# Top-k attention and a leaky-ReLU layer on one core: the sign bit of the weights' rounding on GpSimd, early units transposed on TensorE, and a chunk's first layer begun ahead

## The chip, the cores and the metric

The kernel runs on one core of a Trainium2 chip. The metric is the device time of one execution in microseconds, the median of three runs. The profile is of one further execution, recorded instruction by instruction; its span is the time from the first to the last instruction.

## The reference

Eight batches of eight heads, 576 queries and keys of width 64. Each query keeps its 32 largest scores, the rest are masked, and the softmax weighs the values. The heads are put side by side into 4608 tokens of width 512, which go through two layers with a leaky ReLU between them.

```python
scores = scale * np.matmul(q, k.transpose(0, 1, 3, 2))          # scale = 1/8
kth = np.partition(scores, -32, axis=-1)[..., -32:-31]
scores = np.where(scores >= kth, scores, -1e9)
attn = softmax(scores)                                          # + 1e-9 in the divisor
x = (attn @ v).transpose(0, 2, 1, 3).reshape(4608, 512)
h = x @ w_in                                                    # 512 -> 2048
out = np.maximum(0.01 * h, h) @ w_out                           # 2048 -> 512
```

The two weight matrices come as 64-bit floats; everything else is 32-bit.

## The kernel before

**Rounding the weights.** The weights are loaded as sixteen pieces of 128 x 1024 numbers of four 16-bit words each (tile `raw`, three buffers, issued on the SP queue, L102) and rounded to 32-bit floats on the chip. `round_weights` (L104) is a generator in three stages, and the driver (L484 on) runs stage one of piece n, stage two of piece n-1 and stage three of piece n-2 in turn. Stage one: GpSimd copies the top word out (`top`, L119, two buffers), ScalarE turns the middle and the low words into floats (L120, L122). Stage two: VectorE makes the exponent in `scale` (L124, L126), ScalarE shifts it into place (L128; for the last two pieces VectorE, L130), VectorE makes the top part of the mantissa (`m_top`, in a buffer of the tile `wT`, L131) and keeps the sign bit alone in `top` (L132); TensorE sums the three parts in PSUM (L142 to L144). Stage three: VectorE joins exponent and sign (L146) and multiplies (L149). The loads of the first queries and keys stand between those of the pieces in the SP queue. Top-k of the first unit follows the last piece on VectorE.

**Attention.** Two heads make a pair, four pairs a batch. A unit is 128 rows of queries of one pair (both heads), or, for the 64 rows left over, of two pairs; there are 144 units. A step s works on several units at once: top-k of unit s on VectorE (`top_k`: L244, then four rounds of MAX8 at L249 and of match and replace at L252), the mask of unit s-1 on GpSimd (`mask`: L260, L262, L263), its exponentials and row sums on ScalarE (L266, L271), the reciprocals of unit s-2 on VectorE (L275), its normalizing on ScalarE (L278) and its transposition, and every second step the scores of units s+2 and s+3 on TensorE (`scores`: L214, copied out by ScalarE at L221). Each engine works through its instructions in the order in which the program issues them.

A unit is transposed in one of two ways. `transpose` has ScalarE split the words into two tiles (`split`, L287, two buffers), which go out to DRAM (`apart`, L288) and come back by a transposing DMA (L290). `transpose_in_haste` does nine TensorE transposes into two buffers of the PSUM tile `wide` (L300), which ScalarE copies to `wT` (L306); this is for the units in HURRIED, 15, 23 and 31. The values of two units are weighed together on TensorE (L327), at the place that `values_at` names: step n+4, MIDDLE, for an odd unit n below 14 and its even neighbour, step n+3, END, for later ones, one step sooner for those in HURRIED. ScalarE copies the result into `x` (L341).

**The two layers.** Tokens go in chunks: two of 128, then seventeen of 256. A chunk becomes ready at the place where the values of its last unit are copied. `mlp` (L366) is a generator that yields a cost after every few products. For the 128-token chunks `hidden_of_few` (L345) computes the first layer with the tokens stationary, in four blocks of 512 (L352), and turns each block with four transposes after the next block (L362). For the others the first layer is eight times two tiles of 128 hidden units, each summed over the four pairs (L378), with the activation on ScalarE (L384). The second layer is L390. `mlp_steps` pulls products out of the generators up to a budget, in seven slots of each step (EARLY_SHARE = 500 a slot until the first 256-token chunk is ready, later the backlog spread over the steps until the next chunk is ready). So the feed-forward products are laid between the attention products in TensorE's order.

The units of batch 0 go by query tile first, then by pair. So units 0 to 3 complete the first chunk, 4 to 7 the second, 8 to 15 the third, which is the first of 256 tokens.

```python
            late = s < HURRY and not {s - 1, s - 2} & set(HURRIED)
            if older and not late:
                weights_of(older)
            mlp_steps(budget)
            weighed = values(s, MIDDLE)
```

`weights_of` is the reciprocals and the normalizing; with `late` they come one slot of top-k later.

Of the kernel before, what the change touches and what calls it, by code (L numbers as in the profile page):

```python
# [19 lines left out]
def kernel(  # L20
# [73 lines left out]

    def load_weights(n):
        if n >= NPIECE:
            return
        if not AS_WORDS:
            nc.sync.dma_start(piece(n), weights[n])
            return  # L100
        raw_of[n] = raws.tile([P, WCH, 4], U16, name="raw")
        nc.sync.dma_start(raw_of[n].rearrange("p n w -> p (n w)"), weights[n])  # L102

    def round_weights(n):  # L104
# [14 lines left out]
        nc.gpsimd.tensor_copy(top, raw[:, :, 3])  # L119
        nc.scalar.activation(dst, mid, AF.Copy, bias=-7.0 - 2.0 ** -16, scale=2.0 ** -20)  # L120

        nc.scalar.activation(m_low, low, AF.Copy, bias=128.0, scale=2.0 ** -29)  # L122
        yield
        nc.vector.tensor_scalar(scale, top, 4, 0x7FF, ALU.logical_shift_right, ALU.bitwise_and)  # L124

        nc.vector.tensor_scalar(scale, scale, 1151.0, 896.0, ALU.min, ALU.max)  # L126
# [5 lines left out]
        nc.vector.tensor_scalar(top, top, 0x8000, None, ALU.bitwise_and)  # L132
# [13 lines left out]
        nc.vector.tensor_tensor(scale, scale, top, ALU.bitwise_or)  # L146
# [42 lines left out]
    for b in range(B):  # L189
        first = b % 2 == 1  # L190
        whole = [Unit(b, [b * HP + hp], q0 + LEFT * first)
                 for q0 in range(0, S - LEFT, P) for hp in range(HP)]
# [30 lines left out]
    def first_scores(u):  # L223

        ps = [ps_sc.tile([P, 2, 512], F32, name="wide", bufs=2) for i in range(2)]
        for half in range(2):
            for i, pi, side, r0 in u.parts:
                qt, kt = qk_of[pi]
                d = slice(side * D, (side + 1) * D)
                nc.tensor.matmul(ps[i][:, half, 0:HS], qt[d, u.q0:u.q0 + P],  # L230
# [114 lines left out]
    def hidden_of_few(x):  # L345

        g_of = {}
        for j in range(NFC // 4 + 1):
            if j < NFC // 4:
                ph = ps_ml.tile([P, 512], F32, name="ph", tag="ml")  # L350
                for c in range(HP):
                    nc.tensor.matmul(ph, x[c][:, 0:P], w_in[c][:, j * 512:(j + 1) * 512],  # L352
                                     start=(c == 0), stop=(c == HP - 1))
                    if c == 1:
                        yield 2 * 512
                g_of[j] = raws.tile([P, 2 * DMODEL], U16, name="scale", bufs=2).bitcast(F32)
                nc.scalar.activation(g_of[j], ph, AF.Prelu, alpha=SLOPE)
                yield 2 * 512
            if j:
                pt = ps_ml.tile([P, 4, P], F32, name="pt", tag="ml")  # L360
                for i in range(4):
# [270 lines left out]
```

## Time and profile before

| | us |
|---|---|
| median of three runs | 1476.7 (1475.35 to 1476.87) |
| the profiled execution, its span | 1473.8 |
| TensorE busy with products | 1393.5 |
| VectorE busy | 1328.3 |
| ScalarE, GpSimd busy | 1096.2, 1097.7 |
| first top-k instruction (L244) | 68.7 |
| last VectorE instruction (L275) | 1395.4 |
| products after the last values (L378, L390) | 1414.9 to 1473.8 |

A product of 32-bit floats is two records in the trace. In a stretch without waits, records of L378 start 0.219 us apart, those of L390 and L352 0.429 us. The recorded end of a matmul is modelled, so busy time of TensorE includes some waiting.

In the lines of the profile, a group reads: source line, engine, operation, output <- inputs, shapes and count, then busy time and the mean of one in ns, then idle time of the engine just before these instructions with what ended it. A piece of the chain reads: start, duration, engine, output and line.

### The profile page before, as it was taken

To read this page: it belongs to the slowest core of one execution; us is meant where nothing else is said; L and a number is where in the kernel's file an instruction comes from. 1 tells how busy PE (TensorE), PEld (TensorE's weight loads), DVE (VectorE), ACT (ScalarE), POOL (GpSimd) and SP (SyncE) were. 2 spreads that over 40 slices of the span, in tenths; PEclk is the share of its full clock that TensorE was granted. 3 is DMA by queue.
4 is the path that set the end of the run, shared out by engine and by line. 5 is a ranking of instruction groups with operands and counts; after the bars stand their busy time and mean duration, and the time that the engine had idled before them with its cause. 6 is when DMAs were issued, how large, how long until landed. Compare 5 with 4: busy or idle time off the path is not lost.

```text
span 1473.8 us, 24093 instructions
## 1 busy us (share of the span) xinstructions
PE 1393.5 (95%) x8057; PEld 927.6 (63%) x8059; DVE 1328.3 (90%) x3414; ACT 1096.2 (74%) x1979; POOL 1097.7 (74%) x742
## 2 busy tenths in 40 slices
PE   6716989999999999999999999999999999999998
PEld 2304547676766666666666666767676767676674
DVE  7999999999999999999999999999999999999600
ACT  8647887777787777777777777787877787877710
POOL 2278887888788888788878887888788888787700
PEclk9957999999999999999999999999999999999999
DMA  9724453655367554666466545565557555554510
GB/s 331 298 64 127 131 153 102 175 157 148 105 166 206 142 146 129 180 181 150 135 167 189 155 125 147 165 196 142 130 165 207 138 141 132 165 135 135 144 47 14
DMA packets 391421, 223.48 MB, mean 152 GB/s; under 512 B 336256, under 2 KB 336257, under 8 KB 389249
## 3 DMA queue, kind: packets, MB, share of 16 engines
q1 hardware_dynamic: 391296, 221.95, 53.6%
q8 instruction: 63, 1.03, 0.3%
q14 instruction: 62, 0.50, 0.1%
HBM read 46.14 MB, written 92.60 MB: 94 GB/s over the span
## 4 chain that ended last, share of the span: by engine, by line
PE 81%; DVE 14%; DMA 2%; ACT 2%; issue 1%; SPq 0%; POOL 0%; DVEq 0%; ACTq 0%
PE pz L390 31%; PE ph L378 30%; PE wide L327 10%; PE wide L214 6%; DVE tops L249 5%; DVE pairs L252 4%; PE narrow L214 3%; DVE pairs L244 1%; DMA wT<-apart 1%; ACT split L287 1%; DVE w_out L149 1%; DVE w_in L149 1%; DVE scale L146 1%; DVE scale L124 0%; ACT s_sb L278 0%
## 5 line engine op out<-in xcount | busy, mean ns | idle before, releaser
L262 POOL TENSOR_SCALAR pen<-s_sb,tops 128x576 f32<-128x576 f32 x288 | 638.3, 2216 | 207.7 <-DVE tops L249 120.2
L249 DVE MAX8 tops<-pairs 128x8 f32<-128x288 f32 (+1 forms) x1152 | 635.9, 591 | 0.0
L390 PE MATMUL pz<-w_out,gT 128*128 128x512 f32 x1152 | 508.4, 596 | 0.0
L378 PE MATMUL ph<-x,w_in 128*128 128x256 f32 x2176 | 481.1, 381 | 0.0
L252 DVE MATCH_REPLACE8 pairs<-tops,pairs 128x288 f32<-128x288 f32 (+1 forms) x864 | 460.1, 538 | 0.0
L378 PEld LDWEIGHTS ph<-x,w_in 128*128 128x128 f32 x2176 | 410.7, 190 | 77.1 <-issue 22.9
L263 POOL TENSOR_TENSOR s_sb<-s_sb,pen 128x576 f32<-128x576 f32 x288 | 406.9, 1413 | 24.0
L390 PEld LDWEIGHTS pz<-w_out,gT 128*128 128x128 f32 x1152 | 215.3, 190 | 265.8 <-issue 264.8
L287 ACT COPY split<-s_sb 128x1152 uint16<-128x1152 uint16 x282 | 309.1, 1145 | 0.0
L278 ACT ACTIVATE s_sb<-s_sb,rz 128x576 f32<-128x576 f32 x288 | 207.0, 769 | 38.7 <-DVE rz L275 38.5
L266 ACT ACTIVATE s_sb<-s_sb,nbias 128x576 f32<-128x576 f32 x288 | 221.0, 767 | 12.5 <-POOL s_sb L263 12.5
L244 DVE TENSOR_TENSOR pairs<-s_sb 128x576 f32<-128x576 f32 x288 | 213.6, 780 | 9.9
L327 PEld LDWEIGHTS wide<-wT,vt 128*64 128x64 f32 x3200 | 161.7, 139 | 67.4 <-ACT s_sb L221 26.5
L327 PE MATMUL wide<-wT,vt 128*64 128x128 f32 (+1 forms) x3200 | 179.9, 269 | 24.6 <-ACT s_sb L221 22.3
L384 ACT ACTIVATE gT<-ph 128x512 f32<-128x512 f32 x136 | 80.6, 593 | 80.0 <-PE ph L378 80.0
L341 ACT COPY x<-wide 128x128 f32<-128x128 f32 (+1 forms) x160 | 32.1, 260 | 131.5 <-PE wide L327 131.4
L221 ACT COPY s_sb<-wide 128x704 f32<-128x704 f32 x142 | 107.0, 754 | 23.2 <-PE wide L214 23.1
L214 PE MATMUL wide<-kt,qt 64*128 64x352 f32 (+1 forms) x392 | 75.8, 500 | 26.0 <-ACT s_sb L221 23.6
L221 ACT COPY s_sb<-narrow 128x448 f32<-128x448 f32 x142 | 68.7, 536 | 1.3 <-PE narrow L214 0.7
L397 ACT COPY o_sb<-pz 128x512 f32<-128x512 f32 x36 | 21.1, 585 | 59.4 <-PE pz L390 59.4
L275 DVE RECIPROCAL rz<-ze 128x2 f32<-128x2 f32 x144 | 22.3, 155 | 44.8 <-ACT ze L271 44.7
L252 DVE MATCH_VALUE_LOAD pairs<-tops,pairs 128x8 f32 x864 | 62.5, 72 | 0.0
(62 smaller groups left out, 622.7 us busy)
## 6 DMA issues: line engine op xcount, KB each, us to landing
apart<-split SPq DMA_DIRECT2D x282, 288.0 KB, 2.1
raw<-in_weights_dram SPq DMA_DIRECT2D x16, 1024.0 KB, 6.9
vt<-in_vk_dram SPq DMA_DIRECT2D x32, 320.0 KB, 3.4
out_dram<-o_sb SPq DMA_DIRECT2D x36, 256.0 KB, 2.0
qt<-in_qT_dram SPq DMA_DIRECT2D x20, 288.0 KB, 3.2
kt<-in_kT_dram SPq DMA_DIRECT2D x20, 288.0 KB, 3.6
raw<-in_qT_dram SPq DMA_DIRECT2D x12, 288.0 KB, 3.2
raw<-in_kT_dram SPq DMA_DIRECT2D x12, 288.0 KB, 3.7
```

What stands on the lines that cost most here:

```text
L214: nc.tensor.matmul(to[r0:r0 + u.rows, i, :], qt[d, u.q0:u.q0 + u.rows], kt[d, k0:k1], start=True, stop=True)
L244: nc.vector.tensor_tensor(pairs[:, :, n, :], u.both[:, :, 0:HS], u.both[:, :, HS:S], op)
L249: nc.vector.max(out=u.tops[:, i, r, :], in_=rest[i])
L252: nc.vector.match_replace(out=rest[i], in_to_replace=u.tops[:, i, r, :], in_values=rest[i], imm_value=LOWEST)
L262: nc.gpsimd.tensor_scalar(pen, u.s[i], u.tops[:, i, ROUNDS - 1, 7:8], MASKED, ALU.is_lt, ALU.mult)
L263: nc.gpsimd.tensor_tensor(u.s[i], u.s[i], pen, ALU.add)
L266: nc.scalar.activation(u.s[i], u.s[i], AF.Exp, bias=u.nbias[:, i:i + 1], scale=SCALE, accum_out=u.z[:, i:i + 1])
L278: nc.scalar.activation(u.s[i], u.s[i], AF.Copy, bias=0.0, scale=u.rz[:, i:i + 1])
L287: nc.scalar.copy(split, pairs[:, :, h])
L327: nc.tensor.matmul(po[side * D:(side + 1) * D, o, :], vt[:, c, side, :], u.wT[:, c + side * NKC if c + 1 < NKC else c, r:r + n], start=(c ...
L378: nc.tensor.matmul(ph[:, i, 0:n], w_in[c][:, f * P:(f + 1) * P], x[c][:, 0:n], start=(c == 0), stop=(c == HP - 1),)
L390: nc.tensor.matmul(pz[0:m, 0:DMODEL], gT[:, f, r0:r0 + m], w_out[f // 4][:, f % 4, :], start=(f == 0), stop=(f == NFC - 1),)
```

## The change

- `round_weights`: the sign is no longer cut out of `top` by VectorE. GpSimd makes it from the raw top word with a comparison and a multiplication into a buffer of the tile `split`.
- The first piece is loaded, and its first operations are done, in two halves.
- Units of batch 0: the third and fourth query tiles (units 8 to 15) go pair by pair, both tiles of a pair one after the other.
- HURRIED gains units 3 and 7, whose pairs' values are weighed at END of steps 5 and 9. The new HASTY names the units transposed on TensorE: 0, 1, 2, 3, 7, 14 besides 15, 23, 31. In steps 5, 9 and 17 the reciprocals and the normalizing stand ahead of the step's first slot.
- `begin_hidden`: for the first 256-token chunk, the first eight of sixteen hidden tiles are summed over pairs 0 and 1 from the place where unit 11's values are copied, and over pair 2 from that of unit 13. The sums stay in PSUM, in `narrow` and two `ml` buffers; `mlp` adds pair 3. In step 16 the scores of the next units are made by `first_scores`, which uses `wide` alone.
- In `hidden_of_few` a block is turned later, the last one in the midst of the second layer. Values weighed at MIDDLE are copied earlier in the step. EARLY_SHARE is 490.

```diff
+        sign = work.tile([P, 2 * S], U16, name="split", bufs=2)[:, 0:WCH]
+        for at in parts_of(n):
+            nc.gpsimd.tensor_copy(top[:, at], raw[:, at, 3])
...
+        nc.gpsimd.tensor_scalar(sign, raw[:, :, 3], 32768.0, 32768.0, ALU.is_ge, ALU.mult)
         yield
...
-        nc.vector.tensor_scalar(top, top, 0x8000, None, ALU.bitwise_and)
...
-        nc.vector.tensor_tensor(scale, scale, top, ALU.bitwise_or)
+        nc.vector.tensor_tensor(scale, scale, sign, ALU.bitwise_or)
...
+        tiles = [(0,), (P,), (2 * P, 3 * P)] if b == 0 else [(q0,) for q0 in range(0, S - LEFT, P)]
         whole = [Unit(b, [b * HP + hp], q0 + LEFT * first)
-                 for q0 in range(0, S - LEFT, P) for hp in range(HP)]
+                 for q0s in tiles for hp in range(HP) for q0 in q0s]
...
+    def begin_hidden(ch, pairs):
+        n = CHUNKS[ch]
+        x = x_of[ch]
+        if ch not in begun:
+            first = ps_sc.tile([P, 2, 512], F32, name="narrow").rearrange("p h (f n) -> p h f n", n=CHMAX)
+            begun[ch] = [first[:, 0], first[:, 1]]
+            begun[ch] += [ps_ml.tile([P, 2, CHMAX], F32, name="ph", tag="ml") for k in range(2)]
+        done = 0
+        for f in range(NFC // 2):
+            for c in pairs:
+                nc.tensor.matmul(begun[ch][f // 2][:, f % 2, 0:n], w_in[c][:, f * P:(f + 1) * P], x[c][:, 0:n],
+                                 start=(c == 0 and f % 2 == 0), stop=False)
...
-    HURRIED = (15, 23, 31)
+    HURRIED = (3, 7, 15, 23, 31)
+    HASTY = (0, 1, 2, 3, 7, 14, 15, 23, 31)
...
-        if n < UNHURRIED:
-            return (n | 1) + LAG + 1, MIDDLE
-        return (n | 1) + LAG - ((n | 1) in HURRIED), END
+        if (n | 1) in HURRIED:
+            return (n | 1) + LAG - 1, END
+        return ((n | 1) + LAG + 1, MIDDLE) if n < UNHURRIED else ((n | 1) + LAG, END)
...
+        for last, pairs in ((11, (0, 1)), (13, (2,))):
+            if values_at(last) == place:
+                ready.append(begin_hidden(EARLY, pairs))
...
-    EARLY_SHARE = 500
+    EARLY_SHARE = 490
...
+            at_first = s < HURRY and s - 2 in HURRIED
+            if at_first:
+                weights_of(older)
             slot()
...
-            if s - 2 in HURRIED:
+            if s - 2 in HASTY:
                 transpose_in_haste(older)
...
-                keep_transposed(older) if s - 2 in HURRIED else transpose(older)
+                keep_transposed(older) if s - 2 in HASTY else transpose(older)
+            if not at_once:
+                keep(weighed, s, MIDDLE)
...
-                scores(new)
+                if s == 16:
+                    first_scores(new[0])
+                    first_scores(new[1])
+                else:
+                    scores(new)
```

## The prediction

> **What bounds the kernel now.** The chain of waits comes first, since it says who sets the end:
>
> ```profile
> PE 81%; DVE 14%; DMA 2%; ACT 2%; issue 1%; SPq 0%; POOL 0%; DVEq 0%; ACTq 0%
> ...
> 196.39 0.86 DVE pairs L252 x2
> ...
> 199.55 2.10 ACT split L287 x2
> 201.65 0.50 ACT scale L357
> 202.19 0.85 PE pt L362 x4
> ...
> 325.05 4.50 DMA wT<-apart
> ```
>
> Up to 197 us the chain lies on VectorE (rounding to 68.7, then top-k), from 202 on TensorE, nearly without a break. So the end is the time at which TensorE becomes saturated plus the products then left; and whatever moves VectorE's start at 68.7 moves everything behind it. Busy time by stage (columns: stretch, its length, PE, PEld, DVE, ACT and POOL busy with counts, PE clock, DMA share, GB/s) shows where TensorE has room:
>
> ```profile
> 70.00:130.00 60.00, 14.80 (x100) 10.58 (x96) 59.51 (x158) 33.57 (x61) 45.13 (x31) 0.64 0.30 79
> 130.00:200.00 70.00, 64.82 (x332) 35.70 (x332) 69.45 (x183) 58.00 (x110) 59.95 (x40) 0.95 0.50 139
> 200.00:240.00 40.00, 36.74 (x265) 23.15 (x267) 39.69 (x104) 29.14 (x57) 33.47 (x22) 0.96 0.34 97
> 404.00:1400.00 996.00, 995.78 (x5948) 680.62 (x5949) 946.29 (x2464) 784.97 (x1445) 808.43 (x539) 1.00 0.58 156
> ```
>
> TensorE is idle 45 of 60 us before 130, little after, never after 404. The groups of VectorE say what its lag costs, over the whole span and in 203 to 404 us alone:
>
> ```profile
> L275 DVE RECIPROCAL rz<-ze 128x2 f32<-128x2 f32 x144 | 22.3, 155 | 44.8 <-ACT ze L271 44.7
> ...
> L275 DVE RECIPROCAL rz<-ze 128x2 f32<-128x2 f32 x22 | 3.4, 153 | 7.1 <-ACT ze L271 7.1
> ```
>
> A late TensorE holds back ScalarE's activations, these the row sums, and these VectorE: 7.1 us lost by 404, the other 37.6 later. For the rounding I read VectorE's groups between 10 and 60 us, POOL's groups, and POOL in order of time:
>
> ```profile
> L149 DVE TENSOR_TENSOR w_in<-wide,scale 128x1024 f32<-128x1024 f32 x8 | 9.8, 1224 | 1.2 <-PE wide L144 0.5
> L146 DVE TENSOR_TENSOR scale<-scale,top 128x1024 uint16<-128x1024 uint16 x13 | 8.9, 685 | 0.0
> L126 DVE TENSOR_SCALAR scale<-scale 128x1024 uint16<-128x1024 uint16 x14 | 6.0, 427 | 0.5
> L124 DVE TENSOR_SCALAR scale<-top 128x1024 uint16<-128x1024 uint16 x14 | 6.0, 427 | 2.4 <-POOL top L119 1.0
> L131 DVE TENSOR_SCALAR wT<-top 128x1024 uint16<-128x1024 uint16 x14 | 5.9, 419 | 0.0
> L132 DVE TENSOR_SCALAR top<-top 128x1024 uint16<-128x1024 uint16 x13 | 5.6, 427 | 0.4
> ...
> L262 POOL TENSOR_SCALAR pen<-s_sb,tops 128x576 f32<-128x576 f32 x288 | 638.3, 2216 | 207.7 <-DVE tops L249 120.2
> ...
> 8.21 1.35 POOL L119 COPY top<-raw 128x1024 uint16<-128x1024 uint16 x1 [1.35 <-DMA raw<-in_weights_dram]
> ...
> 23.63 1.13 POOL L119 COPY top<-raw 128x1024 uint16<-128x1024 uint16 x1 [2.59 <-DVE scale L146]
> 27.34 1.12 POOL L119 COPY top<-raw 128x1024 uint16<-128x1024 uint16 x1 [2.59 <-DVE scale L146]
> ```
>
> A piece takes 27.34 - 23.63 = 3.71 us, and VectorE has no idle time to speak of: it is the bound. POOL works 1.13 us of it.
>
> [...] the copy at 8.21 us, beside 0.37 us of L132, took 1.35 us where the later ones, beside L149 alone, took 1.12 to 1.14: 0.22 lost of 0.37. [...] between 70 and 130 us the granted clock was 0.64, so work moved there begins slowly, but in idle time.
>
> **The change, part by part.**
>
> *Sign bit.* L132 goes from VectorE: 0.43 us and 0.02 of gap. In the first two pieces VectorE waits for data anyway, so 14 x 0.45 = 6.3 us. ScalarE (L120, L122, L128 start about 1.05 us apart, 3.15 a piece) allows the new 3.27, barely. Three buffers of raw give a load 3 x 3.27 = 9.8 us; ScalarE and POOL hold one for 2.4, and loads behind the qt and kt pairs in SP's queue landed 7.1 to 8.1 us after their issue (39.67 to 47.00, 43.38 to 51.45), so up to 0.7 us is missing: I leave 5.5 us. The price is POOL's new pass over the same 1024 strided elements, S. Behind it in POOL's queue stands the next piece's copy, for which VectorE's L124 waits; and raw is freed, so the load three pieces on issued, only when it is done. The trace has no such operation. From below: the copy of the same view, 1.1 us. [...] From above: L262's rate, 3.85 ns x 1024 = 3.9 us, or 3.77 with its fixed 0.23 (L260) taken apart. POOL then needs 1.13 + S [...]. With S = 1.1 that is 3.0, hidden, gain 5.5; [...] with 3.77 it is 5.67, loss 28. [...] the operands are immediates and the view is the copy's: **3.5 us gained**. L262 speaks against it and is the rival below.
>
> *First piece in two halves.* The first half can land 1.2 us sooner, but piece 1 (second DMA) doesn't, and L124 and L126 run twice: nothing, VectorE being short of data there.
>
> *Units 0, 1, 2, 3, 7 and 14 transposed on TensorE.* Each gains 9 transposes at 109 ns (the nine of L300 took 0.98 us): 6 x 0.98 = 5.9 us of TensorE, most of it in the idle 70 to 130. ScalarE loses two split copies (2.10 us) and gets two copies of 1.18; SP loses three DMA issues a unit, and with them the two transfers' 2.5 (apart at 594) and 4.6 us (wT, median). So values for units 0 to 3 are complete in step 5 instead of 7, for 4 to 7 in step 9 instead of 11: the two 128-token chunks (29 us of TensorE each) start some 15 us earlier.
>
> *Chunk 2 begun early.* 8 tiles x 3 pairs = 24 products of two records at 0.219 us: 10.5 us moved ahead of the place where the chunk was ready (step 17). There is room: steps 6 to 17 hold about 6 us of feed-forward, 1.2 of values and 1.1 of scores in the 8.87 us that VectorE takes for a step.
>
> But those 10.5 us do not come off the end one for one. A chunk of 256 tokens is spread over the steps until the next is ready. Before, the window of chunk 2 (steps 18 to 25) holds 55 us / 8 + 2.24 of attention = 9.1 us a step, over VectorE's 8.87; after, 44.5 / 8 + 2.24 = 7.8, and TensorE idles 1 us a step, for chunk 3 isn't ready. What is won is the wait that this window caused. VectorE's steps 19, 20 and 24 (9.71, 10.75 and 9.32 us by its L244 starts) lost 3.2 of the 7.1 us; steps 28, 30 and 35 lost the rest, with TensorE 8 us behind by then. Starting that window without a lag should take away a third to a half of the latter. **4.5 us gained**, between 2 (only waits like that for wT at 325 remain) and 10.5.
>
> *Reciprocals to the head of steps 5, 9 and 17.* In step 5 of before the sums come 1.2 us after the head (ze at 113.98, step at 112.77), and all of top-k queues behind the reciprocal. But they are late because the reciprocals of the step before stood 4.5 us into it, ahead of two splits; those now stand at 3.0 and the splits are gone. **0.5 us lost**, 0 to 4.
>
> *At no cost:* turned() moved one block on (its wait of 3.9 us for scale at 202 goes; counted above), the earlier x copies, and the scores of units 18 and 19 in two halves, whose buffers wait for ScalarE some 1 us in step 16, two steps before top-k wants them.
>
> Sum against the profiled 1473.8: -3.5 - 4.5 + 0.5 = -7.5, 1466.3 us. The runs' median of 1476.7 lies 2.9 above that span, so **1469**; with the part ranges 1464 to 1473.
>
> **Rivals.** *POOL becomes the bound of the rounding (slower).* S at L262's rate makes a piece 4.9 us [...]: 14 x 1.2 = 17 or 28 us later at 68.7, all of which VectorE and TensorE inherit. Less 4 us: **1490 to 1501**. For it: the one measured operation of this kind; against: it reads 4-byte data and a threshold per partition. It decides from S = 2.1 on, where the start loses the 4 us that the rest gains. *POOL takes just what VectorE gives* (S near 1.8): only the second part remains, **1473**. *All the moved work counts*, if TensorE's lag, not its load in one window, is what lasts: -5.5 - 10.5, **1461**; against it the 7.8 us a step.
>
> **How the numbers follow.** Forecast 0.42, all counts 0.10, takes what it gives 0.18, POOL bound 0.30. A measurement can tell 0.2%, 3 us. Faster: 0.42 + 0.10 + 0.15; same 0.04; slower 0.29. The range runs from inside the third case, 1458, to 1493, which leaves out the upper half of the POOL case.
>
> **What would show it.** First top-k instruction at 64 to 66 us (right), 69 (takes what it gives), 85 or more (POOL); the sign row's mean under 1.8 us; VectorE's idle before the reciprocals, up to 404 us, at 2 to 4 instead of 7.1; idle TensorE between 230 and 290; the same 9.2 us a step after 500. I am wrong if the sign operation takes over 2 us, or if TensorE has no room in steps 6 to 17 and chunk 2 starts late.

## The result, and the profile after

| | before | after |
|---|---|---|
| median of four runs, us | 1476.8 (1475.35 to 1476.93) | 1493.3 (1490.90 to 1497.58) |
| the profiled execution, its span | 1473.8 | 1491.1 |
| first top-k instruction | 68.7 | 84.0 |
| span less first top-k | 1405.1 | 1407.1 |

After stands to before as 1.0117 (95% interval 1.0093 to 1.0141): slower, where I had forecast 1469. The two spans differ by 17.3 us, of which 15.3 arise before top-k begins and 2.0 after it. The second part of the change, from which I expected the larger gain, gained nothing. In what follows, a ratio is against runs of the kernel before on the same chip (their medians lie between 1474.7 and 1476.7 us), with its 95% interval.

The chain of waits on the page of the kernel after:

```profile
PE 77%; DVE 9%; DMA 4%; ACT 4%; POOL 2%; issue 2%; SPq 0%; DVEq 0%; POOLq 0%; ACTq 0%
```

VectorE's share has fallen from 14 to 9% and POOL has 2%: during the rounding POOL leads now. POOL's groups, the sign line among them, and then POOL in order of time:

```profile
L274 POOL TENSOR_SCALAR pen<-s_sb,tops 128x576 f32<-128x576 f32 x288 | 638.3, 2216 | 209.9 <-DVE tops L261 127.9 <-ACT s_sb L278 40.7 <-ACT s_sb L290 19.8
...
L132 POOL TENSOR_SCALAR split<-raw 128x1024 uint16<-128x1024 uint16 x16 | 59.1, 3691 | 0.1
...
L128 POOL COPY top<-raw 128x1024 uint16<-128x1024 uint16 x15 | 16.7, 1114 | 0.0
```

```profile
24.69 1.14 POOL L128 COPY top<-raw 128x1024 uint16<-128x1024 uint16 x1
25.78 3.69 POOL L132 TENSOR_SCALAR split<-raw 128x1024 uint16<-128x1024 uint16 x1
29.41 1.12 POOL L128 COPY top<-raw 128x1024 uint16<-128x1024 uint16 x1
```

The sign pass takes 3.691 us, three times the copy of the same words, and POOL has no idle time before either. A piece takes 29.41 - 24.69 = 4.72 us, where VectorE had needed 3.71. VectorE between 10 and 60 us:

```profile
L135 DVE TENSOR_SCALAR scale<-top 128x1024 uint16<-128x1024 uint16 x11 | 14.4, 1306 | 9.5 <-POOL top L128 9.5
L159 DVE TENSOR_TENSOR w_in<-wide,scale 128x1024 f32<-128x1024 f32 x8 | 9.8, 1225 | 1.3 <-DVE scale L156 0.5
L156 DVE TENSOR_TENSOR scale<-scale,split 128x1024 uint16<-128x1024 uint16 x10 | 6.8, 684 | 0.0
L137 DVE TENSOR_SCALAR scale<-scale 128x1024 uint16<-128x1024 uint16 x10 | 4.3, 427 | 0.3
L142 DVE TENSOR_SCALAR wT<-top 128x1024 uint16<-128x1024 uint16 x10 | 4.2, 420 | 0.0
```

It now waits 9.5 us for the copy of the top word, which stands behind the sign pass of the piece before. L135 also takes 1.306 us, where the same operation before took 0.427. That is 0.88 us a piece on VectorE, double what the removed 0.43 us had cost, though it doesn't decide here, since VectorE waits for POOL in any case.

Busy time by stage, stretches moved on by the 15.3 us of the later start (columns as before: stretch, length, PE, PEld, DVE, ACT, POOL, clock, DMA share, GB/s), and VectorE's reciprocals over the whole span and in the 201 us that answer to 203 to 404 of before:

```profile
85.30:145.30 60.00, 29.67 (x182) 19.74 (x180) 59.55 (x158) 30.88 (x64) 45.19 (x32) 0.69 0.00 1
145.30:215.30 70.00, 64.75 (x322) 34.73 (x321) 69.29 (x183) 57.61 (x110) 59.90 (x40) 0.98 0.45 118
419.30:1415.30 996.00, 994.16 (x5943) 679.60 (x5944) 946.70 (x2464) 784.09 (x1443) 808.67 (x539) 1.00 0.58 156
```

```profile
L287 DVE RECIPROCAL rz<-ze 128x2 f32<-128x2 f32 x144 | 22.4, 155 | 47.1 <-ACT ze L283 46.9
...
L287 DVE RECIPROCAL rz<-ze 128x2 f32<-128x2 f32 x22 | 3.4, 153 | 7.5 <-ACT ze L283 7.5
```

TensorE did work 29.7 us of the first 60 instead of 14.8, so the earlier chunks and the transposes did move into idle time. But VectorE's wait for the row sums is 7.5 us, where it was 7.1 before and I had looked for 2 to 4.

To see where the time went I counted TensorE's products at their unhindered spacing (0.219 us for a record of 256 columns, 0.429 for one of 512, and so on) in each step of VectorE, and took the rest of the step as idle. Steps are reckoned from the first top-k, so the late start is left out:

| | before | after |
|---|---|---|
| TensorE idle up to the end of step 18, us | 64.0 | 51.3 |
| idle in steps 19 to 25 | 1.6 | 9.1 |
| idle up to the end | 84.1 | 80.2 |
| VectorE's step 19 takes | 9.71 | 12.21 |
| VectorE's step 26 begins at | 233.6 | 234.7 |

By the end TensorE is idle 84.1 - 80.2 = 3.9 us less and does 5.9 us more work, the transposes; 5.9 - 3.9 = 2.0, the loss found above. Of the 12.7 us of idle time saved by step 18, 7.5 come back in the next seven steps.

### The profile page after: what moved, and what is told of

Same layout as the page of the kernel before. It is cut to its first block, busy times and chain, and to the rows that moved or that the text cites. A ratio compares the mean times of both kernels' runs of the same rounds, so it can differ in the third digit from the quotient of the medians.

```text
span 1491.1 us, 24200 instructions
## 1 busy us (share of the span) xinstructions
PE 1409.7 (95%) x8113; PEld 934.1 (63%) x8113; DVE 1335.6 (90%) x3400; ACT 1092.7 (73%) x1981; POOL 1154.9 (77%) x759
## 4 chain that ended last, share of the span: by engine, by line
PE 77%; DVE 9%; DMA 4%; ACT 4%; POOL 2%; issue 2%; SPq 0%; DVEq 0%; POOLq 0%; ACTq 0%
PE ph L419 28%; PE pz L431 28%; PE wide L339 10%; PE wide L226 6%; DVE tops L261 3%; PE narrow L226 3%; DVE pairs L264 3%; DMA wT<-apart 2%; POOL split L132 2%; ACT split L299 2%; DMA apart<-split 1%; ACT s_sb L290 1%; DVE pairs L256 1%; ACT s_sb L278 1%; POOL top L128 1%
## 5 line engine op out<-in xcount | busy, mean ns | idle before, releaser
L419 PE MATMUL ph<-x,w_in 128*128 128x256 f32 x2120 | 469.4, 381 | 0.0
L419 PEld LDWEIGHTS ph<-x,w_in 128*128 128x128 f32 x2120 | 399.9, 190 | 75.9 <-issue 23.1
L299 ACT COPY split<-s_sb 128x1152 uint16<-128x1152 uint16 x270 | 295.9, 1144 | 0.0
L290 ACT ACTIVATE s_sb<-s_sb,rz 128x576 f32<-128x576 f32 x288 | 207.0, 769 | 34.1 <-DVE rz L287 34.1
L339 PEld LDWEIGHTS wide<-wT,vt 128*64 128x64 f32 x3200 | 158.4, 137 | 51.6 <-ACT ze L283 18.2
```

What stands on the lines that cost most here:

```text
L290: nc.scalar.activation(u.s[i], u.s[i], AF.Copy, bias=0.0, scale=u.rz[:, i:i + 1])
L299: nc.scalar.copy(split, pairs[:, :, h])
L339: nc.tensor.matmul(po[side * D:(side + 1) * D, o, :], vt[:, c, side, :], u.wT[:, c + side * NKC if c + 1 < NKC else c, r:r + n], start=(c ...
L419: nc.tensor.matmul(ph[:, i, 0:n], w_in[c][:, f * P:(f + 1) * P], x[c][:, 0:n], start=(c == 0), stop=(c == HP - 1 and (i == 1 or not first)),)
```

## Experiments on the sign bit

**The sign bit back, the rest as after.**

```diff
-        nc.gpsimd.tensor_scalar(sign, raw[:, :, 3], 32768.0, 32768.0, ALU.is_ge, ALU.mult)
...
+        nc.vector.tensor_scalar(top, top, 0x8000, None, ALU.bitwise_and)
...
-        nc.vector.tensor_tensor(scale, scale, sign, ALU.bitwise_or)
+        nc.vector.tensor_tensor(scale, scale, top, ALU.bitwise_or)
```

> The changed kernel with the sign bit cut out by VectorE again; halves of the first piece, order of units, transposes and early sums stay. Theory A (the sign pass on GpSimd is all of the loss; the rest of the change nets to about 2 us of loss, because it adds 5.9 us of transposes to TensorE and what it moves ahead comes back as idle time in the window of chunk 2): first top-k instruction near 68, time 1476 to 1479, idle TensorE in steps 18 to 25 about 8 us more than before. Theory B (the schedule does gain the 4.5 us forecast, and the sign costs some 21): time 1470 to 1473. Theory C (the schedule itself costs much, the sign only part): 1482 or more.

Measured: 1478.5, 1.0019 of before (1.0011 to 1.0026). First top-k is back at 68.94. So the sign bit carries nearly the whole loss, and the rest of the change by itself is a small loss of 2.8 us, not a gain of 4. The halves of the first piece are in this kernel and its first top-k is not sooner than before's 68.69: they do nothing, as forecast. Single executions of this kernel spread from 1476.3 to 1484.6 us (before: 1475.0 to 1478.1), and the profiled one took 1483.9, so the stalls in its trace are larger than in most; where a stall is compared below, the trace of the kernel after stands beside it, which has the same schedule.

**The sign bit alone.** The kernel before with the sign made on GpSimd, otherwise unchanged.

> The kernel before with the sign bit made on GpSimd, nothing else of the change. Theory A: a piece takes GpSimd 1.1 + 3.7 = 4.8 us against 3.72, the first top-k instruction comes at 84 to 86, and all that follows is shifted by it: 1491 to 1494. Theory B: as the sign costs some 21, 1497 or more. Theory C: 1482 to 1488.

Measured: 1492.1, 1.0108 (1.0094 to 1.0122), first top-k at 84.16. Undone and done alone, it gives the same 15 us.

**What GpSimd's passes cost.** Nine forms of one pass, run twice in a loop after the last mask, when VectorE has finished (the loop and its buffers are not shown).

```diff
+            nc.gpsimd.tensor_scalar(o16, probe[:, :, 3], 32768.0, 32768.0, ALU.is_ge, ALU.mult)
+            nc.gpsimd.tensor_scalar(o16, flat[:, 0:WCH], 32768.0, 32768.0, ALU.is_ge, ALU.mult)
+            nc.gpsimd.tensor_scalar(o16, probe[:, :, 3], 32768.0, None, ALU.is_ge)
+            nc.gpsimd.tensor_scalar(o16, probe[:, :, 3], 2.0, None, ALU.mult)
+            nc.gpsimd.tensor_copy(o16, probe[:, :, 3])
+            nc.gpsimd.tensor_scalar(o32, words[:, 0:S], 0.5, 2.0, ALU.is_lt, ALU.mult)
+            nc.gpsimd.tensor_scalar(o32, words[:, 0:S], 2.0, 1.0, ALU.mult, ALU.add)
+            nc.gpsimd.tensor_scalar(o32, words[:, 0:S], 2.0, None, ALU.mult)
+            nc.gpsimd.tensor_copy(o32, words[:, 0:S])
```

> The kernel before with nine forms added on GpSimd, each twice, behind its last mask, where the engine has nothing left to do: the sign pass as in the change (two-byte, every fourth word, compare and multiply), the same on contiguous words, with the comparison alone, with a multiplication alone, and the copy of that view; and on 576 four-byte numbers compare and multiply with immediates, multiply and add, multiply alone, and a copy. Theory P1 (a tensor-scalar costs GpSimd some 3.6 ns an element whatever its operations, type and stride): 3.7 us for all on 1024 elements, 2.2 on 576, copies 1.1 and less. P2 (the comparison is what costs): 3.7 for the three with a comparison, 1.1 to 1.9 for a multiplication alone. P3 (the second operation costs): the one-operation forms at half. The time stays within 1 us of the kernel before.

POOL in order of time, the second round (lines 580 to 588 are the nine forms in the order of the diff):

```profile
1425.28 3.71 POOL L580 TENSOR_SCALAR split<-raw 128x1024 uint16<-128x1024 uint16 x1
1429.07 3.63 POOL L581 TENSOR_SCALAR split<-raw 128x1024 uint16<-128x1024 uint16 x1
1432.78 2.83 POOL L582 TENSOR_SCALAR split<-raw 128x1024 uint16<-128x1024 uint16 x1
1435.69 2.83 POOL L583 TENSOR_SCALAR split<-raw 128x1024 uint16<-128x1024 uint16 x1
1438.59 1.10 POOL L584 COPY split<-raw 128x1024 uint16<-128x1024 uint16 x1
1439.65 2.15 POOL L585 TENSOR_SCALAR pen<-raw 128x576 f32<-128x576 f32 x1
1441.88 0.67 POOL L586 TENSOR_SCALAR pen<-raw 128x576 f32<-128x576 f32 x1
1442.63 1.66 POOL L587 TENSOR_SCALAR pen<-raw 128x576 f32<-128x576 f32 x1
1444.35 0.66 POOL L588 COPY pen<-raw 128x576 f32<-128x576 f32 x1
```

The sign pass takes its 3.7 us with VectorE silent (3.71 here, 3.691 in the kernel after), so it is not slowed by a neighbour. Its stride costs 0.08 us (L580 against L581). Neither the comparison nor the immediates nor the word size change it by more than a tenth: one operation costs 2.8 to 2.9 ns an element (L582, L583, L587), two cost 3.5 to 3.7 (L580, L581, L585), L262 with its threshold per partition 3.85, and a comparison takes the 2.83 us that a multiplication does. The one exception is multiplication and addition together (L586), 1.16 ns, which is the price of the copy (L588, 1.15). None of the three explanations that I had set down was right as it stood.

**Two fast passes.** That exception can make a sign bit: scale the word so that it rounds to 0 or 1, then multiply by 32768.

```diff
+        nc.gpsimd.tensor_scalar(sign, raw[:, :, 3], 2.0 ** -15, 2.0 ** -17 - 0.5, ALU.mult, ALU.add)
+        nc.gpsimd.tensor_scalar(sign, sign, 32768.0, 0.0, ALU.mult, ALU.add)
...
-        nc.vector.tensor_scalar(top, top, 0x8000, None, ALU.bitwise_and)
...
-        nc.vector.tensor_tensor(scale, scale, top, ALU.bitwise_or)
+        nc.vector.tensor_tensor(scale, scale, sign, ALU.bitwise_or)
```

> The kernel before, with the sign bit made on GpSimd by two multiply-and-add passes instead of one comparison-and-multiplication (the first scales the word to 0 or 1 by rounding, the second multiplies by 32768). Theory A (the loss is the duration of GpSimd's pass, by its form, and nothing else of moving the sign): two passes at 1.1 to 1.2 us each make a piece on GpSimd 3.4 us, less than VectorE's 3.3 to 3.7, so first top-k stands at 63 to 66 us instead of 68.7 and the time is 1471 to 1474. Rival P (VectorE's first exponent operation takes 1.3 us whenever GpSimd works beside it, as in the kernel after): the piece is 4.1 us on VectorE, first top-k at 74 to 76 us, 1481 to 1484.

Measured: 1492.6, 1.0109 (1.0095 to 1.0122), as slow as the slow pass. POOL, and then VectorE, in order of time in the same stretch:

```profile
25.80 1.04 POOL L125 TENSOR_SCALAR split<-split 128x1024 uint16<-128x1024 uint16 x1
26.78 1.28 POOL L120 COPY top<-raw 128x1024 uint16<-128x1024 uint16 x1
29.37 1.14 POOL L124 TENSOR_SCALAR split<-raw 128x1024 uint16<-128x1024 uint16 x1 [1.31 <-DVE scale L148]
```

```profile
25.94 1.18 DVE L127 TENSOR_SCALAR scale<-top 128x1024 uint16<-128x1024 uint16 x1
27.15 1.20 DVE L129 TENSOR_SCALAR scale<-scale 128x1024 uint16<-128x1024 uint16 x1
28.27 0.41 DVE L134 TENSOR_SCALAR wT<-top 128x1024 uint16<-128x1024 uint16 x1
28.61 0.68 DVE L148 TENSOR_TENSOR scale<-scale,split 128x1024 uint16<-128x1024 uint16 x1
29.39 1.23 DVE L151 TENSOR_TENSOR w_in<-wide,scale 128x1024 f32<-128x1024 f32 x1
30.72 1.20 DVE L127 TENSOR_SCALAR scale<-top 128x1024 uint16<-128x1024 uint16 x1
```

The passes are fast (1.04 and 1.14 us), and POOL now waits for VectorE: 1.31 us a piece. But L127 begins 0.14 us after L125 and ends at 27.12, 0.28 us after L125's end; L129 ends 0.29 us after the end of L120. Both take 1.2 us instead of 0.43, so a piece on VectorE takes 30.72 - 25.94 = 4.78 us. POOL's three passes fill 3.4 us of each piece, and only L151, with one operand in PSUM, lies beside one of them undisturbed (1.224 us on average, as L149 before). Rival P had the cause and less than half the size: two instructions are held up, not one. Theory A falls.

**The sign bit fused on VectorE.** Another way to drop the instruction: one operation that cuts the sign out of `top` and joins it.

```diff
-        nc.vector.tensor_scalar(top, top, 0x8000, None, ALU.bitwise_and)
...
-        nc.vector.tensor_tensor(scale, scale, top, ALU.bitwise_or)
+        nc.vector.scalar_tensor_tensor(scale, top, 0x8000, scale, ALU.bitwise_and, ALU.bitwise_or)
```

> The kernel before, in which VectorE cuts out the sign and joins it to the exponent in one instruction (scalar_tensor_tensor: top and 0x8000, or scale), so that the separate cut of 0.43 us is gone and GpSimd gets nothing. If the fused instruction takes the 0.69 us of the join: a piece 3.27 us, first top-k instruction at 62 to 64, time 1470 to 1472. [...] a piece 3.8, first top-k instruction at 70, 1477 to 1478.

Measured: 1479.1, 1.0020 (1.0013 to 1.0026). VectorE's groups between 10 and 60 us:

```profile
L145 DVE SCALAR_TENSOR_TENSOR scale<-top,scale 128x1024 uint16<-128x1024 uint16 x13 | 15.9, 1220 | 0.9 <-ACT scale L128 0.7
```

1.22 us replace 0.43 + 0.69: fused is dearer than apart, the second of my two cases. First top-k comes at 71.29, 2.6 us late, and the time rises by 2.9: a microsecond at the start costs about a microsecond at the end.

## Experiments on the schedule

**Without the early sums.** The run with the sign bit back, and `begin_hidden` is never called.

```diff
-        for last, pairs in ((11, (0, 1)), (13, (2,))):
-            if values_at(last) == place:
-                ready.append(begin_hidden(EARLY, pairs))
```

> The changed kernel with the sign back on VectorE (1478.5) and without the early sums of chunk 2: its 24 products are made in its own window. Theory A (what is moved ahead only leaves TensorE idle later): 1477 to 1480. Rival B (the early sums gain, something else in the schedule loses): 1483 or more. Rival E (they hurt, since they delay chunk 2's first tiles): 1475.5 or less.

Measured: 1483.2, 1.0042 (1.0028 to 1.0055). So the early sums are worth some 3 us against the schedule without them, and the schedule without them has lost some 6 against before: rival B.

**Work left out altogether.** If moving 10.5 us ahead is worth little, how much is it worth to remove them? In the kernel before, eight hidden tiles of chunk 2, and in another run of chunk 10, are summed over pair 3 alone. The lines that open a sum, pace the products and reckon their cost change along with it (not shown); for the other run, 2 is 10.

```diff
-                for c in range(HP):
+                for c in range(HP - 1 if ch == 2 and f < NFC // 2 else 0, HP):
```

> The kernel before, in which chunk 2 (the first of 256 tokens) leaves out the 24 products that the change moves ahead (tiles 0 to 7 of the first layer, pairs 0 to 2), 10.5 us of TensorE; its output differs there. It bounds from above what moving them can gain. Theory A (a window's load counts only as far as it makes VectorE wait; TensorE idles for the rest until the next chunk is ready): 1472 to 1475. Rival D (TensorE is saturated from 203 us on, so work taken away anywhere shortens the end by itself): 1466.

> The same 24 products left out of chunk 10 instead of chunk 2; its output differs there. Theory A: in the saturated part TensorE enters the window some 6 us behind VectorE and a window makes VectorE wait 3 us, so more of the 10.5 us counts than in chunk 2: 1468 to 1472. Rival D: 1466 for both chunks alike.

Measured: 0.9994 (0.9986 to 1.0002) for chunk 2, 0.9985 (0.9977 to 0.9993) for chunk 10. Of 10.5 us of work, 0.9 and 2.2 us show. With chunk 2 relieved TensorE's idle time had risen by 9.5 us by step 26, the end of its window. My expectations had put too much on both, even those of theory A.

**Fewer transposes on TensorE.** The run with the sign bit back, with units 0, 1, 2 and 14 transposed by DMA again.

```diff
-    HASTY = (0, 1, 2, 3, 7, 14, 15, 23, 31)
+    HASTY = (3, 7, 15, 23, 31)
```

> The changed kernel with the sign back on VectorE (1478.5), in which units 0, 1, 2 and 14 are transposed by DMA again and only 3 and 7 remain on TensorE beside the three of before: 3.9 us of TensorE less. Theory A (they lie in idle time of TensorE, and cost nothing): 1477.5 to 1479.5. Rival F (TensorE is the bound, so each costs its length): 1474.5. Against both, if unit 2 comes too late for step 5: 1480 or more.

Measured: 1478.8, 1.0018 (1.0012 to 1.0025), as with them (1.0019). These four lie in idle time, as forecast.

**More transposes on TensorE.** The run with the sign bit back, with units 18 to 22, 24 and 25 transposed on TensorE as well (23 was already).

> The kernel after, sign bit on VectorE again, and units 18 to 25 too are transposed on TensorE. Theory G (what the schedule gains for TensorE is lost in TensorE's waits, in order, for wT to come back by DMA around the change from chunk 2 to chunk 3): VectorE's stall of 3 us at steps 26 and 27 vanishes, the time falls from 1478.5 to 1475 to 1476.5. Rival N (the stall has another cause, such as ScalarE's order): VectorE's steps 26 to 28 lose as before, 1478 to 1480.

Measured: 1483.4, 1.0044 (1.0030 to 1.0058). Neither expectation: VectorE's stall at step 26 is 0.8 us, where the sign bit back had 3.0 and the kernel after 1.2, but step 24 lost 1.9 instead. TensorE's waits for `wT` between steps 19 and 28 (4.2 us in the kernel after) are gone. But the 7 x 0.98 us of added transposes lie where TensorE has little room, and some half of them show in the time.

**A larger share for the early products.** The run with the sign bit back, and:

```diff
-    EARLY_SHARE = 490
+    EARLY_SHARE = 600
```

> The kernel after, sign bit on VectorE again, and EARLY_SHARE 600 instead of 490, so that the two 128-token chunks are computed sooner and chunk 2 begins with no lag. Theory L (chunk 2's first product comes 2.4 us later against VectorE's steps than it should, because the early products fill steps 13 to 17): the stalls of steps 19 and 20 shrink by 2 us or more and the time is 1474.5 to 1477. Rival W (time freed for TensorE there comes back as idle time, as in the runs that left work out): 1478 to 1479.5, with steps 26 on as before.

Measured: 1481.3, 1.0035 (1.0022 to 1.0048). Neither again: against before, VectorE loses 4.4 us in steps 10 to 12 and 2.7 in 16 and 17, where the early products stand ahead of attention's, and gains back 4.3 by step 36.

**What a window can gain.** Chunks 3 to 16 of the kernel before are made lighter by the same amount each: two hidden tiles, or eight, summed over pair 3 alone (the lines that open a sum, pace the products and reckon their cost change too, not shown).

```diff
+                light = 3 <= ch <= 16 and f in LIGHT      # (0, 8), or every even tile
-                for c in range(HP):
+                for c in range(HP - 1 if light else 0, HP):
```

> The kernel before, but each of chunks 3 to 16 leaves out 6 of its first layer's products (two of sixteen hidden tiles are summed over pair 3 alone; the output differs): 2.63 us of TensorE less in each of 14 windows of eight steps, 36.8 us in all. Theory M (in each window the slower of TensorE's load, 9.19 us a step, and VectorE's 8.87 counts, and no window's slack passes to the next): 2.5 us gained a window, 35 in all, about 1442; with stalls of single steps left over, up to 1452. Rival Q (VectorE's lost time in the windows is from stalls of order, not of load): under 10 us gained, 1467 or more.

> The kernel before, but each of chunks 3 to 16 leaves out 24 of its first layer's products (eight of sixteen hidden tiles are summed over pair 3 alone; the output differs): 10.5 us of TensorE less in each of 14 windows, 147 us in all. Theory M: no more than the run with 2.63 us a window gains, but for its left-over stalls, 1438 to 1445. Rival C (work taken from TensorE counts in full, as the prediction's third rival had it): 1330. Rival Q: as the two runs that left it out of one chunk, 1.1 to 1.9 us a window, 1450 to 1461.

Measured: 1451.1, 0.9840 (0.9826 to 0.9853), and 1436.3, 0.9744 (0.9729 to 0.9759): 23.6 and 38.4 us gained for 36.8 and 147 us of work. The reciprocals of VectorE between 404 and 1204 us, before and with 10.5 us a window less, and the page's chain of the latter:

```profile
L275 DVE RECIPROCAL rz<-ze 128x2 f32<-128x2 f32 x108 | 16.8, 156 | 30.5 <-ACT ze L271 30.3
```

```profile
L275 DVE RECIPROCAL rz<-ze 128x2 f32<-128x2 f32 x112 | 17.2, 153 | 0.1
```

```profile
DVE 74%; PE 17%; issue 5%; ACT 2%; DMA 1%; DVEq 0%; POOL 0%; SPq 0%; ACTq 0%
```

VectorE waits for nothing any more, its steps from 26 to 138 fall from 9.186 to 8.872 us, its own pace, and the chain lies on it. That is 35.2 us over fourteen windows, 2.5 a window, though 10.5 are taken away; the rest of the 38.4 comes behind step 138. With 2.63 us taken away the steps fall to 8.960, 1.8 us a window. This fits theory M, that in each window the slower of the two engines counts and what lies above that is lost, if not exactly: the larger gain is 1.7 us beyond its range, and the smaller lies at the end that it allows for left-over stalls. Rivals C and Q fall.

**What stalls step 19.** In the kernel after, TensorE, ScalarE and VectorE at the start of chunk 2's window, in order of time:

```profile
249.98 1.13 PE L419 MATMUL narrow<-x,w_in 128*128 128x256 f32 x4 [0.53 <-ACT x L353]
251.15 0.60 ACT L425 ACTIVATE gT<-narrow 128x512 f32<-128x512 f32 x1 [1.22 <-PE narrow L419]
...
251.80 1.13 PE L419 MATMUL narrow<-x,w_in 128*128 128x256 f32 x4 [0.69 <-ACT gT L425]
...
252.97 0.60 ACT L425 ACTIVATE gT<-narrow 128x512 f32<-128x512 f32 x1 [1.22 <-PE narrow L419]
253.83 0.60 ACT L425 ACTIVATE gT<-ph 128x512 f32<-128x512 f32 x1 [0.27 <-PE ph L419]
254.33 1.43 ACT L290 ACTIVATE s_sb<-s_sb,rz 128x576 f32<-128x576 f32 x2
...
260.12 0.17 DVE L287 RECIPROCAL rz<-ze 128x2 f32<-128x2 f32 x1 [3.17 <-ACT ze L283]
```

Since three pairs are summed already, a block of two hidden tiles needs only 1.1 us of TensorE before its activation. Two such blocks lie in the tile `narrow`; TensorE's sum into the second waits for ScalarE's activation of the first, and the activation for the sum. The normalizing (L290) stands behind three activations in ScalarE's order, the exponentials and row sums behind it, and VectorE waits 3.17 us for these. How long step 19 takes varies by about 1 us between runs that are alike up to there: 9.6 to 10.7 us in the traces with the order of before, 10.5 to 13.9 with early sums and a share of 490. I tried three edits, each with the sign bit back: chunk 2 laid half a step later; the four products into `narrow` laid together ahead of both activations; and both.

```diff
             if at == place:
+                backlog[0] += mlp_cost(ch)
+            if (at if ch != EARLY else (at[0] + 1, MIDDLE)) == place:
                 ready.append(mlp(ch))
-                backlog[0] += mlp_cost(ch)
```

> The kernel after, sign bit on VectorE again, and the remaining products of chunk 2 are laid into TensorE's order half a step later (from MIDDLE of step 18 instead of END of step 17). Theory L (ScalarE's activations of chunk 2 stand in its queue ahead of the exponentials while TensorE still works on the transposes and values of steps 15 to 17, and VectorE's stall of 2.4 us at step 19 follows from that): the stall at step 19 falls below 1 us and the time from 1478.5 to 1475.5 to 1477. Rival W (the stall comes from the products of the window themselves, and only moves): some step between 18 and 22 still loses 2 us or more, 1478 to 1480.

```diff
+            both = first and f0 < 4
-            for i in range(2):
+            for i in range(4 if both and f0 == 0 else 0 if both else 2):
...
+                to = begun[ch][i // 2] if both else ph
```

> The kernel after, sign bit on VectorE again, and the four products that complete the two halves of the tile narrow stand together, ahead of both their activations. Theory N (the stall at step 19 is a ping-pong: in the kernel after TensorE's second sum into narrow waited 0.69 us for ScalarE's activation of the first, and each of ScalarE's two activations waited 1.22 us for TensorE, with the normalizing and the exponentials queued behind): these waits go, VectorE's stall at step 19 falls from 2.4 to 1 us or less, and the time from 1478.5 (1.0019 of before) to 0.9995 to 1.001 of before. Rival K (the eight short activations of chunk 2 in the window's first two steps are too many for ScalarE, whatever their order): a stall of 2 us or more stays, 1.0015 of before or more.

> As the run that completes narrow in one go, and chunk 2's remaining products half a step later as well. Theory N: in the run with the later place alone TensorE's second sum into narrow waited 3.55 us for the first activation, which had a split in front of it; with one go this wait cannot arise, the stall at step 19 falls to 1 us or less, 0.999 to 1.0005 of before. Rival K: a stall of 2 us or more at step 19 or 20, 1.0015 of before or more.

Measured: 1.0017 (1.0009 to 1.0025), 0.9998 (0.9990 to 1.0006) and 0.9996 (0.9988 to 1.0004). Half a step later alone doesn't help: step 19 still takes 12.17 us, and the trace shows why, the activation now having a split in front of it:

```profile
238.82 0.60 ACT L424 ACTIVATE gT<-narrow 128x512 f32<-128x512 f32 x1
...
239.46 2.07 PE L418 MATMUL narrow<-x,w_in 128*128 128x256 f32 x4 [3.55 <-ACT gT L424]
```

With the products in one go this wait is gone, and the ratio falls from 1.0019 to 0.9998, with intervals that don't meet. The first lines of that kernel there:

```profile
234.88 1.99 PE L420 MATMUL narrow<-x,w_in 128*128 128x256 f32 x8 [0.53 <-ACT x L352]
236.71 4.68 PE L420 MATMUL ph<-x,w_in 128*128 128x256 f32 x20
236.91 1.09 ACT L426 ACTIVATE gT<-narrow 128x512 f32<-128x512 f32 x2 [2.08 <-PE narrow L420]
```

Step 19 still takes 11.35 us there, more than theory N allowed, so a stall stays, as rival K had it, though the time is theory N's; against the kernel after, only 0.8 us of the gain arises at step 19, and 1.2 at step 26. The clearer pair is that of the two runs with the later place: laying the products in one go shortens step 19 from 12.17 to 8.93 us, and these 3 us stay to the end (1.0017 against 0.9996). VectorE's groups for the reciprocals in the stretch from 200 to 424 us, with the later place alone and with both edits:

```profile
L286 DVE RECIPROCAL rz<-ze 128x2 f32<-128x2 f32 x24 | 3.7, 155 | 6.9 <-ACT ze L282 6.9
```

```profile
L286 DVE RECIPROCAL rz<-ze 128x2 f32<-128x2 f32 x25 | 3.8, 151 | 3.4 <-ACT ze L282 3.3
```

With both edits VectorE begins step 36 4.0 us sooner than before, as much as I had forecast for the whole of this part. By step 140 only 1.2 are left: 0.6 us go at step 52, 0.8 at 70, 1.0 at 102 and 1.4 at 124 and 126, of which 0.8 are regained between. TensorE's waits for a DMA between 330 and 1400 us tell what goes with this; before, and with both edits (engine and line, what it waited for, us in total, times, the longest):

```profile
PE wide L327 <- DMA wT<-apart: 0.9, 1, 0.9
```

```profile
PE wide L338 <- DMA wT<-apart: 3.5, 6, 0.8
```

TensorE comes to the values of a pair, in its order, before `wT` is back by DMA. Four of the six waits lie in steps 69, 101, 123 and 125, each one step ahead of one of VectorE's stalls, and the 2.6 us more of waiting nearly match the 2.8 that are lost. Why `wT` comes too late there, and not before, no run shows. This kernel is the best version found, and it equals before within the measurement.

**Is it just the laying?** One constant of the laying changed, in the kernel before and in the run without early sums (490 and 500 exchanged).

> The kernel before with EARLY_SHARE 490 instead of 500 and nothing else: the same work, laid a few products later or sooner from step 6 on. Theory D (the order in which products fall between attention's operations shifts the later stalls by some us whichever part is changed, which is why the run without early sums lies at 1.0042 though its VectorE starts lie within 0.4 us of before up to step 30): the ratio leaves 1 by 0.0015 to 0.004, either way. Rival Z (such a small shift is absorbed): within 0.001 of before, and what the run without early sums loses comes from its transposes or its order of units.

> The run without early sums (sign bit on VectorE), with EARLY_SHARE 500 instead of 490. Theory D: its ratio moves by 0.0015 or more from 1.0042, either way. Rival Z: 1.0035 to 1.005.

Measured: 1.0005 (0.9998 to 1.0011) and 1.0037 (1.0023 to 1.0052). Rival Z holds both times: such a shift is absorbed, and what the run without early sums loses belongs to the other edits in it. TensorE's waits in that run with 500, between 330 and 1400 us as above:

```profile
PE wide L338 <- DMA wT<-apart: 5.9, 10, 1.2
```

That is 5.0 us more than before, and VectorE, 0.5 us behind before at step 30, is 6.8 behind at its last step, both reckoned from the first top-k. Eight of the ten waits lie one step ahead of a stall of VectorE.

## Why the prediction was wrong

**Sign bit: the failed step.** I had put S under 1.8 us, on the ground that "the operands are immediates and the view is the copy's". That was an estimate of mine, and no trace of this case had shown it. S measured 3.69 us, more than three times the copy's 1.13 and within 3% of the 3.77 us that I had worked out from L262's rate and made a rival. The rival's smaller figure for a piece was 4.9 us (measured 4.72), and its range of 1490 to 1501 holds the result, by some luck: it counts 17 us for the start, where 15.3 came, and 4 gained by the schedule, which didn't come. The objections to L262 were both void: in the table of passes immediates, word size and stride change nothing beyond a tenth (3.54 to 3.85 ns an element for two operations, L262's included). A measured row of the same instruction form should have been the likeliest value and the copy's the other end. This one choice is 15.3 us of the 17.3, and, as I had 3.5 gained for it, 18.8 of the 24.8 us by which the forecast span and the measured one differ.

**What GpSimd takes from VectorE.** I reckoned what three of VectorE's instructions (1.28 us) take from POOL at the rate at which the copy at 8.21 us had lost time beside L132, 0.22 us of 0.37: 0.77 us a piece, an estimate. It is in the pieces of 3.0 and 5.67 us and in the 28 us, not in the 4.9 and the 17. For what POOL takes from VectorE I reckoned nothing. VectorE pays more: 0.88 us a piece on L135, 1.5 with two fast passes. So even S = 1.1, which I put down as a gain of 5.5 us, would probably have lost: one instruction held up for 0.77 us, as each of the two was, makes VectorE's piece 3.71 - 0.45 + 0.77 = 4.03 us, an estimate that no run tests by itself. With two fast passes the loss is 16 us.

**Chunk 2 begun early: the schedule is wrong in sign, by some 7 us.** "4.5 us gained", 4.0 with the reciprocals' loss, measures 2.8 lost when the sign bit is taken out. Three things are in it. A window relieved of 10.5 us of TensorE gives back little: one chunk gave 0.9 and 2.2, and fourteen gave 2.5 each, TensorE's excess over VectorE there. I had written down the 7.8 us a step and the idle microsecond that follow from this, and then added later stalls to the gain. Second, the half summed ahead brings a stall of its own: its activations follow each other at 1.1 us of TensorE, in the same tile, ahead of the normalizing in ScalarE's order. I had costed the early sums by TensorE's time alone and named nothing queued behind their activations; this term is 3 us. Third, I put the rest of the schedule at no cost beyond that half microsecond, and without the early sums it loses 6 us. So the early sums as such do gain 3.4 us, against that worse schedule. Mended, the schedule gives 4.0 us by step 36, more than one window's excess, so a start without lag does reach into the next windows; but most of the lead is gone again by the end, beside TensorE's waits for `wT`. I had named such waits only as the case in which chunk 2 gains 2.

**What held.** Four of the six transposes, of units 0, 1, 2 and 14, cost nothing (1.0018 without them, 1.0019 with). Chunk 2's window idles 1 us a step more (7.5 in seven steps), and is the idle TensorE between 230 and 290 us that I named as a sign. From step 26 to 138 a step takes 9.197 us against 9.186. Work that stands in TensorE's idle stretch does begin slowly: in the kernel after, the nine transposes at 107 us took 2.18 us at a granted clock of 0.50, those at 133 us 1.20 at 1.00. The halves give nothing, though the copy of the first begins 1.0 us sooner (4.72 us against 5.75). The 0.5 us for the reciprocals was not tried by itself, but in the trace of the kernel after VectorE's steps up to 19 begin within 0.2 us of before's, reckoned from the first top-k, so that loss isn't seen.

**What stays open.** Without early sums the schedule part loses 6 us, and neither the share nor a stall up to step 30 explains it (VectorE's starts stand within 0.5 us of before until then). It shows later, beside TensorE's waits for `wT`. Which edit brings these waits on, I have not separated: the transposes of units 3 and 7, the order of units, the later turning of the small chunks' blocks or another of the small edits.

## What to carry to other kernels

Price an operation by the nearest measured row of its own instruction form on its own engine before that of a cheaper form on the same data, and let the objections to that row be tested, not argued. When work goes from VectorE to GpSimd, count what GpSimd's passes do to VectorE's neighbouring instructions too: dropping 0.43 us here cost 0.9 to 1.5. And where two engines share a pipeline cut into windows, work taken out of a window gained here no more than about its excess over the other engine, 2.5 of 10.5 us, while blocks made shorter brought their activations sooner into a queue that others stood in. After such a change, look for the waits that a lead runs into later; here they were for a DMA.

## What the runs showed of the hardware that I had not expected

- GpSimd's tensor-scalar pass: 2.8 ns an element with one operation (2.83 us for 1024, comparison or multiplication), 3.5 to 3.6 with two (3.63 us contiguous, 3.71 strided), 2.9 and 3.7 with 32 bits (1.66 and 2.15 us for 576); multiplication and addition together took the copy's 1.1 to 1.2 ns (0.67 us for 576, the copy 0.66).
- Beside the slow sign pass, VectorE's first 16-bit tensor-scalar took 1.306 us, but the next two, within the same 3.69 us pass, their usual 0.427 and 0.420. So the slow pass did not hold VectorE until its end. Beside the fast passes, of 1.04 to 1.28 us, L127 and L129 took 1.18 and 1.20 us and ended 0.28 and 0.29 us after the pass, while L151, with one operand in PSUM, kept its 1.22. Why the two kinds differ, no run shows.
- VectorE's scalar-tensor-tensor on 16-bit words took 1.22 us for 1024 elements, against 0.69 for tensor-tensor and 0.43 for tensor-scalar.
